# Block 3's statistics on ScalarE, Wv's loads re-cut, evacuations on VectorE and own banks for V in the first segment of a memory-attention and GLU kernel

## The chip, the cores and the metric

One core of a Trainium2 chip runs the kernel. The metric is the device time in microseconds; lower is better. The kernel before ran at 319.13, 319.97 and 320.19 us (median 319.97 us). Its profiled execution took 319.35 us.

Names of engines in the profile: PE is the matrix engine (PEld its weight loads), DVE is VectorE, ACT is ScalarE, POOL is GpSimd, SP issues DMAs. ACT can issue DMAs too (ACTq).

## The reference, cut to what matters

Input x is 2048 tokens by 640 features in bf16. It is normalised over the features, and the result feeds two branches whose outputs are multiplied and added to x:

```
xn = layernorm(x)
# branch A, 32 heads of 20 features, 4 segments of 512 tokens, a memory M, z carried along
q, k, v = xn @ wq, xn @ wk, xn @ wv
per segment: a_dot = softmax(q k^T / sqrt(20) + causal mask) v
             a_mem = phi(q) M / (phi(q) z + 1e-6)
             o     = g * a_mem + (1 - g) * a_dot        # g = sigmoid(beta)
             M += phi(k)^T v ;  z += sum phi(k)
s = o @ wo
# branch B
h = sigmoid(xn @ w_gate) * (xn @ w_up)                  # 640 -> 1536
g = silu(h @ w_down)                                    # 1536 -> 640
out = x + s * g
```

What the change touches is the first step for the first segment alone: the layernorm of its 512 tokens, their transposition, and v = xn @ wv.

## The kernel before, in words

The 2048 tokens are cut into four segments of 512, and each segment into four blocks of 128 tokens (j = 0 to 3; the title's "block 3" is j = 2, "block 4" is j = 3). A tile holds 128 partitions. Matmuls contract over partitions, so each product needs xn transposed: `xnT` holds features on partitions (five chunks of 128) and tokens along the row. A segment needs V (8 products of 128 tokens by 320 columns, five accumulating matmuls each), K and Q (5 products of 128 features by 512 tokens each, again five matmuls each), 12 pairs of gate and up products, scores and attention, and the down products.

For segments 1 to 3 this work is laid into a planner's slots by due times (`TIMES`), far from the change. The first segment's head is written out by hand, in program order, and each engine runs its own instructions strictly in that order. Engines wait for each other through semaphores.

The hand-written head runs as follows (line numbers of the kernel before):

- DMAs are issued from SP and ACT in this order. SP: block 0's left half, block 1, block 2, Wv's right half, Wk, Wq, beta. ACT: block 0's right half, Wv's left half, block 3. Wg and Wu follow on ACT later, in the middle of its work (L144).
- `keep_warm(9)` (L644) runs nine matmuls on zeros while the first block is on its way; a tenth stands after the first transposes.
- For each block: `half_stats0` (L654, L656) is two VectorE `bn_stats` of 320 columns and one `bn_aggr`; the reciprocal standard deviation comes from a ScalarE Sqrt (`root0`, L659) and a VectorE reciprocal (L676) for blocks 0 and 1, and from two GpSimd instructions, add and power (`ln_rstd`, L244 and L245), for blocks 2 and 3; `norm0` (L249) is one VectorE instruction of 640 columns.
- Block 0 is transposed by `first_transpose` (L667) in two pieces of three and two chunks, copied out of PSUM by ScalarE (L672) and VectorE (L670). Blocks 1 to 3 go through `ln_transpose`: five PE transposes (L263) and one copy of 640 columns, on ScalarE for blocks 1 and 2 (L266), on VectorE for block 3 (L268).
- `do_V` runs five matmuls (L130, tile `psv`) and a ScalarE copy into V (L355).
- Then come K (`do_K`, tile `psq`, evacuated by VectorE), Q, the first gates and the slots.

PSUM has eight banks. `Sps`, the scores, holds four of them from the start; the pool `ps_d` of four banks serves everything else, V's products and the transposes included, and each new tile waits for the release of the one four before it.

Of the kernel before, what the change touches and what calls it, by code (L numbers as in the profile page):

```python
# [9 lines left out]
P = 128  # L10
D = 640
# [4 lines left out]
L = 512  # L16
F = 1536
DC = D // P
# [4 lines left out]
HD = D // 2  # L23
# [58 lines left out]
def kernel(  # L82
# [14 lines left out]
    nc = tc.nc  # L97
# [1 line left out]
    o2 = out.flatten_outer_dims()  # L99

    cpool = ctx.enter_context(tc.tile_pool(name="const", bufs=1))
    ps_s = ctx.enter_context(tc.tile_pool(name="ps_s", bufs=1, space=PSUM))
    ps_d = ctx.enter_context(tc.tile_pool(name="ps_d", bufs=4, space=PSUM))
    lnp = ctx.enter_context(tc.tile_pool(name="ln", bufs=2))
    stg = ctx.enter_context(tc.tile_pool(name="stg", bufs=1))
# [13 lines left out]
    ctx.enter_context(tc.manual_schedule(  # L119
        engines={ENG.PE, ENG.Activation, ENG.DVE, ENG.Pool, ENG.SP}))  # L120

    Sps = ps_s.tile([P, 4, L], F32, name="Sps")

    xt_of, xnT_of = {}, {}

# [11 lines left out]
    def load_x(n, a=0, b=4, cols=slice(0, D), eng=nc.sync):  # L137
        if n not in xt_of:
            xt_of[n] = lnp.tile([P, 4, D], BF, name="xt4", bufs=3)
        src = x2[n * L:(n + 1) * L, :].rearrange("(j p) d -> p j d", p=P)  # L140
        eng.dma_start(xt_of[n][:, a:b, cols], src[:, a:b, cols])
# [13 lines left out]
    nc.vector.memset(warm[:, 0:L], 0.0)  # L155
    beta_b = cpool.tile([P, H], BF, name="beta_b")

    def load_wv(half, eng):
        hs = slice(half * HD, (half + 1) * HD)
        eng.dma_start(Wv[:, :, hs], A_wv[:, hs].rearrange("(c p) n -> p c n", p=P))  # L160


    load_x(0, 0, 1, slice(0, HD))
    load_x(0, 0, 1, slice(HD, D), nc.scalar)
    load_x(0, 1, 2)
    load_wv(0, nc.scalar)
    load_x(0, 2, 3)
    load_x(0, 3, 4, eng=nc.scalar)
    load_wv(1, nc.sync)
    load_w(nc.sync, Wk, A_wk)  # L170
    load_w(nc.sync, Wq, A_wq)
    nc.sync.dma_start(beta_b[:], A_beta.partition_broadcast(P))

    epsc = cpool.tile([P, 2], F32, name="epsc")
    nc.gpsimd.memset(epsc[:], EPS)

    nc.scalar.activation(epsc[:, 1:2], epsc[:, 0:1], ACT.Sqrt)
# [69 lines left out]
    def ln_norm(n, j, mv, rs):  # L247
        xn = lnp.tile([P, D], BF, name="xn", bufs=2)
        nc.vector.tensor_scalar(xn[:], xt_of[n][:, j, :], mv[:, j, 0:1], rs[:, j:j + 1],  # L249
                                op0=ALU.subtract, op1=ALU.mult)  # L250
        return xn
# [3 lines left out]
        rs = lnp.tile([P, 4], F32, name="rs")  # L255
        return mv, rs

    def ln_transpose(n, j, xn, eng):
        if n not in xnT_of:
            xnT_of[n] = xpool.tile([P, DC, L], BF, name="xnT")  # L260
        pT = ps_d.tile([P, DC, P], BF, name="pT", tag="d")
        for c in range(DC):
            nc.tensor.transpose(pT[:, c, :], xn[:, c * P:(c + 1) * P], ident[:])  # L263
        dst = xnT_of[n][:, :, j * P:(j + 1) * P]
        if eng is nc.scalar:
            nc.scalar.copy(dst, pT[:])  # L266
        else:
            nc.vector.tensor_copy(dst, pT[:])  # L268

    def ln_spill(n, j, xn):  # L270
        nc.sync.dma_start(Xd[n % 2][j * P:(j + 1) * P, :], xn[:])

# [71 lines left out]
            nc.sync.dma_start(QT[32 * r + DH:32 * r + DH + 3, 4 * half:4 * half + 4, :],  # L344
                              src[r][:, 4 * half:4 * half + 4, :])

    def do_V(n, j, half, evac):
        ps = ps_d.tile([P, HD], F32, name="psv", tag="d")
        for k in range(DC):
            mm(ps[:], xnT_of[n][:, k, j * P:(j + 1) * P], Wv[:, k, half * HD:(half + 1) * HD],  # L350
               k == 0, k == DC - 1)
        dst = V[n % 2][:, j, half * 16:(half + 1) * 16, 0:DH]
        src = ps[:].rearrange("p (h e) -> p h e", e=DH)
        if evac is nc.scalar:
            nc.scalar.copy(dst, src)  # L355
        else:
            nc.vector.tensor_copy(dst, src)
# [290 lines left out]
    new_seg(0)  # L648
    xns, sts = {}, {}

    def half_stats0(j, i):
        if i == 0:
            sts[j] = lnp.tile([P, 2, 6], F32, name="st")
        nc.vector.bn_stats(sts[j][:, i, :], xt_of[0][:, j, i * HD:(i + 1) * HD])  # L654
        if i == 1:
            nc.vector.bn_aggr(mv[:, j, :], sts[j][:])  # L656

    def root0(j):
# [2 lines left out]
    def first_transpose():  # L661

        xnT_of[0] = xpool.tile([P, DC, L], BF, name="xnT")
        for c0, c1 in ((0, 3), (3, 5)):
            pT = ps_d.tile([P, c1 - c0, P], BF, name="pT", tag="d")
            for c in range(c0, c1):
                nc.tensor.transpose(pT[:, c - c0, :], xns[0][:, c * P:(c + 1) * P], ident[:])  # L667
            dst = xnT_of[0][:, c0:c1, 0:P]
            if c0:
                nc.vector.tensor_copy(dst, pT[:])  # L670
            else:
                nc.scalar.copy(dst, pT[:])  # L672

    def norm0(j):
        if j < 2:
            nc.vector.reciprocal(rs[:, j:j + 1], rs[:, j:j + 1])  # L676
        xns[j] = ln_norm(0, j, mv, rs)

    half_stats0(0, 0)
    half_stats0(0, 1)  # L680
    root0(0)
    half_stats0(1, 0)
    norm0(0)
    half_stats0(1, 1)
    half_stats0(2, 0)
    first_transpose()
    root0(1)
    load_w(nc.scalar, Wg, B_w_gate)
    norm0(1)
    half_stats0(2, 1)  # L690
    ln_rstd(mv, rs, slice(2, 3))
    half_stats0(3, 0)
    half_stats0(3, 1)
    ln_rstd(mv, rs, slice(3, 4))
    norm0(2)
    keep_warm(1)
    do_V(0, 0, 0, nc.scalar)
    ln_transpose(0, 1, xns[1], nc.scalar)
    norm0(3)
    late_constants(xns[3])  # L700
    load_w(nc.scalar, Wu, B_w_up)
    do_V(0, 0, 1, nc.scalar)
    do_V(0, 1, 0, nc.scalar)
    ln_transpose(0, 2, xns[2], nc.scalar)
    do_V(0, 1, 1, nc.scalar)
    ln_transpose(0, 3, xns[3], nc.vector)
    do_V(0, 2, 0, nc.scalar)
    do_V(0, 2, 1, nc.scalar)
    do_V(0, 3, 0, nc.scalar)
    do_V(0, 3, 1, nc.scalar)  # L710
    nc.scalar.activation(epsc[:, 1:2], epsc[:, 0:1], ACT.Tanh)
    for c in range(5):
        do_K(0, c, nc.vector)
# [265 lines left out]
```

## Time and profile before

| | |
|---|---|
| median of three runs | 319.97 us (319.13 to 320.19) |
| profiled execution, its own time | 319.35 us |
| its span, first to last instruction | 317.6 us |
| PE busy | 309.7 us, 98% of the span, 4215 matmuls |
| DVE, ACT, POOL busy | 229.5, 227.2, 135.5 us (72%, 72%, 43%) |
| granted clock of PE, mean | 0.999 |
| first matmul on zeros (L644) | 1.24 us |
| first transpose of block 0 (L667) | 5.30 us |
| first V matmul (L130) | 6.37 us |
| first K matmul | 13.35 us |
| first scores (L548) | 35.68 us |

Times inside an execution are counted from the span's start. In a timeline row the first number is the start, the second the time covered, and in brackets stands how long the engine had been idle and what ended that. A busy PE in the profile is modelled (a matmul's end is set by a model of the pipeline), so that starts of matmuls say more than their durations.

### The profile page before, as it was taken

The page shows a single profiled execution, that of the slowest core. Times are in us where ns is not written, and L with a number is a line of the kernel's source. Part 1 is how long each engine was busy: PE and PEld are TensorE (multiplying, and loading weights), DVE is VectorE, ACT ScalarE, POOL GpSimd, SP SyncE. Part 2 cuts the span into 40 slices and gives each one's busy share as a digit, 9 for nine tenths or more (in the row PEclk, how much of TensorE's full clock was granted, in tenths as well). Part 3 has the DMA queues.
Part 4 walks back from the last instruction along what each step waited for, and adds up shares of the span by engine and source line. Part 5 has one row for each costly group of instructions (what it writes and reads, how often), then busy time and mean ns, then how long its engine had stood idle before and what let it go on. Part 6 is the DMA issues. An engine that isn't in the chain of part 4 may idle for free.

```text
span 317.6 us, 10049 instructions
## 1 busy us (share of the span) xinstructions
PE 309.7 (98%) x4215; PEld 167.1 (53%) x4244; DVE 229.5 (72%) x505; ACT 227.2 (72%) x229; POOL 135.5 (43%) x230
## 2 busy tenths in 40 slices
PE   8999999999999999999999999999999999999995
PEld 3544445665555445654665455545466645445673
DVE  6474356755869888997779999977787686734565
ACT  3723477788898877778898868678897766777631
POOL 1870036535263445334453354444533353535322
PEclk9999999999999999999999999999999999999999
DMA  7984886420752462505954443238533000350302
GB/s 252 364 328 142 289 221 191 105 46 2 215 158 62 130 130 85 126 23 173 240 168 122 114 110 109 82 121 210 168 82 120 19 23 23 114 137 4 99 20 83
DMA packets 56085, 41.36 MB, mean 130 GB/s; under 512 B 26952, under 2 KB 54664, under 8 KB 56040
## 3 DMA queue, kind: packets, MB, share of 16 engines
q1 hardware_dynamic: 53496, 35.97, 39.7%
q10 hardware_dynamic: 2544, 4.75, 4.0%
q8 instruction: 33, 0.54, 0.7%
q14 instruction: 12, 0.10, 0.1%
HBM read 19.90 MB, written 14.78 MB: 109 GB/s over the span
## 4 chain that ended last, share of the span: by engine, by line
PE 96%; issue 1%; ACT 1%; DVE 1%; ACTq 0%
PE yp L130 11%; PE up L130 11%; PE gp L130 10%; PE psq L130 10%; PE Sps L548 9%; PE gp L134 6%; PE up L134 6%; PE yp L134 6%; PE psv L130 6%; PE ApsT L572 5%; PE psq L134 4%; PE sp L130 3%; PE sp L134 3%; PE sp L532 2%; PE psv L134 1%; PE wps L644 1%
## 5 line engine op out<-in xcount | busy, mean ns | idle before, releaser
L556 ACT ACTIVATE pt<-Sps 128x2048 bf16<-128x2048 f32 (+1 forms) x81 | 150.3, 1856 | 40.8 <-PE Sps L548 35.9
L558 POOL TENSOR_SCALAR_AFFINE_SELECT pt<-pt 128x512 bf16<-128x512 bf16 x128 | 83.2, 665 | 157.6 <-ACT pt L556 157.5
L438 DVE SCALAR_TENSOR_TENSOR hT<-tg,up 128x512 bf16<-128x512 bf16 x48 | 32.4, 675 | 23.2 <-PE up L130 8.7
L130 PE MATMUL up<-xnT,Wu 128*128 128x512 bf16 x147 | 40.3, 380 | 1.2 <-issue 1.0
L130 PE MATMUL yp<-Wd,hT 128*128 128x320 bf16 x257 | 40.1, 300 | 0.0
L427 ACT ACTIVATE tg<-gp 128x512 bf16<-128x512 f32 x48 | 28.6, 596 | 14.4 <-PE gp L130 11.0
L130 PE MATMUL gp<-xnT,Wg 128*128 128x512 bf16 x144 | 38.1, 379 | 0.3 <-issue 0.2
L548 PE MATMUL Sps<-QT,KT 23*128 23x128 bf16 (+3 forms) x512 | 32.6, 301 | 0.2
L591 DVE STREAM_TRANSPOSE obT<-ob 128x512 bf16<-128x512 bf16 x30 | 21.1, 705 | 13.4 <-POOL ob L587 13.3
L130 PEld LDWEIGHTS <-hT 128*128 128x128 bf16 x257 | 23.5, 98 | 11.6 <-issue 3.0
L455 DVE SCALAR_TENSOR_TENSOR aa<-t,yp 128x320 bf16<-128x320 bf16 x32 | 15.3, 480 | 13.8 <-ACT t L454 13.7
L134 PE MATMUL gp<-xnT,Wg 128*32 128x512 bf16 x360 | 24.1, 380 | 0.0
L548 PEld LDWEIGHTS <-KT 23*128 23x128 bf16 x512 | 10.0, 92 | 24.5 <-issue 24.1
L130 PEld LDWEIGHTS <-Wu 128*128 128x128 bf16 x160 | 14.3, 98 | 16.2 <-issue 3.2
L593 DVE STREAM_TRANSPOSE tb<-ApsT 128x512 f32<-128x512 f32 x30 | 21.2, 708 | 2.2 <-PE ApsT L572 2.1
L572 PE MATMUL ApsT<-pt,V 128*32 128x512 bf16 (+2 forms) x480 | 22.7, 299 | 0.0
L130 PEld LDWEIGHTS <-Wg 128*128 128x128 bf16 x150 | 14.1, 98 | 16.0 <-issue 1.9
L134 PE MATMUL up<-xnT,Wu 128*32 128x512 bf16 x320 | 21.7, 380 | 0.0
L454 ACT ACTIVATE t<-yp 128x320 bf16<-128x320 f32 x32 | 13.9, 435 | 10.2 <-PE yp L130 8.5
L130 PE MATMUL psv<-Wv,xnT 128*128 128x320 bf16 x130 | 20.6, 299 | 0.2
L587 POOL TENSOR_TENSOR ob<-tb,rb 128x320 bf16<-128x320 f32 x27 | 19.8, 733 | 2.3
L134 PE MATMUL yp<-Wd,hT 128*32 128x320 bf16 x508 | 20.0, 300 | 0.0
(122 smaller groups left out, 448.7 us busy)
## 6 DMA issues: line engine op xcount, KB each, us to landing
KT<-Kd SPq DMA_DIRECT2D x32, 80.0 KB
QT<-Qd SPq DMA_DIRECT2D x32, 80.0 KB
out_dram<-xt SPq DMA_DIRECT2D x14, 160.0 KB
Wg<-in_B_w_gate_dram ACTq DMA_DIRECT2D x1, 1920.0 KB
Wu<-in_B_w_up_dram ACTq DMA_DIRECT2D x1, 1920.0 KB
xt<-in_A_x_dram SPq DMA_DIRECT2D x3, 640.0 KB
Wd<-in_B_w_down_dram SPq DMA_DIRECT2D x1, 1920.0 KB
Xd<-xn SPq DMA_DIRECT2D x12, 160.0 KB
```

The lines of the kernel that those rows point to most:

```text
L130: nc.tensor.matmul(out_, lhsT=lhsT, rhs=rhs, start=start, stop=stop, skip_group_check=True)
L134: nc.tensor.matmul(out_[cols], lhsT=lhsT[:, cols], rhs=rhs, start=start, stop=stop, tile_position=(0, 32 * r), skip_group_check=True)
L427: nc.scalar.activation(tg[:], gp[:], ACT.Tanh, scale=0.5)
L438: nc.vector.scalar_tensor_tensor(out=h[:], in0=seg[n]["tg"][:], scalar=1.0, in1=up[:], op0=ALU.add, op1=ALU.mult)
L455: nc.vector.scalar_tensor_tensor(out=s["aa"][j][:, hs], in0=t2[:], scalar=1.0, in1=yp[:], op0=ALU.add, op1=ALU.mult)
L548: nc.tensor.matmul(Sps[:, r, c0:c0 + ncol], lhsT=KT[32 * r:32 * r + DH + 3, g, kb * P:(kb + 1) * P], rhs=QT[32 * r:32 * r + DH + 3, g, q0: ...
L556: nc.scalar.activation(pt[:, :, 0:ntot], Sps[:, :, 0:ntot], ACT.Exp, scale=SCALE)
L558: nc.gpsimd.affine_select(out=pt[:, :, c0:c0 + P], in_=pt[:, :, c0:c0 + P], compare_op=ALU.is_ge, fill=0.0, base=0, pattern=[[0, 4], [1, P ...
L572: nc.tensor.matmul(ps[32 * r:32 * r + 32, q0:L], lhsT=Vflat[n % 2][:, off:off + 32], rhs=t[:, r, c0:c0 + ncol], start=(i == 0), stop=(i == ...
L587: nc.gpsimd.tensor_tensor(ob[:, :, 0:DH], tb[:, :, 0:DH], rb[:].unsqueeze(2).to_broadcast([P, L // 32, DH]), op=ALU.mult)
L591: nc.vector.transpose(s["obT", g // 4][:, g % 4, :], ob[:].rearrange("p b e -> p (b e)"))
L593: s["turn", g] = (lambda: nc.vector.transpose(tb[:].rearrange("p b e -> p (b e)"), ps[:]), quotients, turn_back)
```

## The change

It touches the first segment's head alone.

1. **Loads.** SP now issues block 0's left half, block 1, chunks 0 to 2 of Wv's left half, block 3, Wv's right half, Wk, Wq, beta. ACT issues block 0's right half, block 2, chunks 3 and 4 of Wv's left half. There is one DMA more.
2. **Block 2's statistics** move from VectorE (two `bn_stats`, one `bn_aggr`) and GpSimd (two instructions) to ScalarE: an Identity pass with scale -1/640 whose row sum is the negative mean, a Square pass with that as bias whose row sum is 640 times the variance, and a Sqrt; VectorE takes the reciprocal and normalises. The passes write to a tile of the `aa` pool that nobody reads. A new tile `sums` (two floats) is allocated behind `epsc`.
3. **Block 3's** reciprocal deviation moves from GpSimd to ScalarE (Sqrt) and VectorE (reciprocal).
4. **Evacuations.** The transposes of blocks 1 and 2 are copied out by VectorE in place of ScalarE. Block 0's two pieces are two chunks (ScalarE) and three (VectorE) in place of three and two. Transposition and evacuation are separate calls, so that they can be placed apart in program order.
5. **PSUM.** V's products in the first segment use four banks of their own (`ps_v`); these are given back before `Sps` is allocated in their place.
6. **Order.** On ScalarE the Identity pass stands ahead of block 0's copy, Square and Sqrt behind block 1's Sqrt and ahead of the issue of Wg; block 3's Sqrt stands ahead of the second V copy, Wu's issue behind it. On VectorE the evacuations of blocks 1 and 2 stand between statistics and norms. On PE only the transposes of block 3 move, behind the first V product of block 2.

```diff
-    ps_s = ctx.enter_context(tc.tile_pool(name="ps_s", bufs=1, space=PSUM))
...
-    Sps = ps_s.tile([P, 4, L], F32, name="Sps")
+    first = ExitStack()
+    ps_v = first.enter_context(tc.tile_pool(name="ps_v", bufs=4, space=PSUM))
...
     load_x(0, 1, 2)
-    load_wv(0, nc.scalar)
-    load_x(0, 2, 3)
-    load_x(0, 3, 4, eng=nc.scalar)
+    load_x(0, 2, 3, eng=nc.scalar)
+    load_wv(0, nc.sync, 0, 3)
+    load_wv(0, nc.scalar, 3, DC)
+    load_x(0, 3, 4)
     load_wv(1, nc.sync)
...
     epsc = cpool.tile([P, 2], F32, name="epsc")
+    sums = cpool.tile([P, 2], F32, name="sums")
...
-        for c0, c1 in ((0, 3), (3, 5)):
+        for c0, c1 in ((0, 2), (2, 5)):
...
+    def act_stats(step):
+        if step == 0:
+            sts[2] = fpool.tile([P, D], BF, name="aa", bufs=4)
+            nc.scalar.activation(sts[2][:], xt_of[0][:, 2, :], ACT.Identity, scale=-1.0 / D,
+                                 accum_out=sums[:, 0:1])
+        elif step == 1:
+            nc.scalar.activation(sts[2][:], xt_of[0][:, 2, :], ACT.Square, bias=sums[:, 0:1],
+                                 accum_out=sums[:, 1:2])
+        else:
+            nc.scalar.activation(rs[:, 2:3], sums[:, 1:2], ACT.Sqrt, scale=1.0 / D, bias=epsc[:, 0:1])
...
     half_stats0(0, 0)
     half_stats0(0, 1)
     root0(0)
+    act_stats(0)
     half_stats0(1, 0)
     norm0(0)
     half_stats0(1, 1)
-    half_stats0(2, 0)
     first_transpose()
     root0(1)
+    act_stats(1)
+    act_stats(2)
     load_w(nc.scalar, Wg, B_w_gate)
     norm0(1)
-    half_stats0(2, 1)
-    ln_rstd(mv, rs, slice(2, 3))
     half_stats0(3, 0)
+    keep_warm(1)
+    do_V(0, 0, 0, nc.scalar, ps_v)
+    transpose0(1)
+    evacuate0(1, nc.vector)
+    norm0(2)
     half_stats0(3, 1)
-    ln_rstd(mv, rs, slice(3, 4))
-    norm0(2)
-    keep_warm(1)
-    do_V(0, 0, 0, nc.scalar)
-    ln_transpose(0, 1, xns[1], nc.scalar)
+    root0(3)
+    do_V(0, 0, 1, nc.scalar, ps_v)
+    load_w(nc.scalar, Wu, B_w_up)
+    do_V(0, 1, 0, nc.scalar, ps_v)
+    transpose0(2)
+    do_V(0, 1, 1, nc.scalar, ps_v)
+    evacuate0(2, nc.vector)
     norm0(3)
     late_constants(xns[3])
-    load_w(nc.scalar, Wu, B_w_up)
-    do_V(0, 0, 1, nc.scalar)
-    do_V(0, 1, 0, nc.scalar)
-    ln_transpose(0, 2, xns[2], nc.scalar)
-    do_V(0, 1, 1, nc.scalar)
-    ln_transpose(0, 3, xns[3], nc.vector)
-    do_V(0, 2, 0, nc.scalar)
-    do_V(0, 2, 1, nc.scalar)
-    do_V(0, 3, 0, nc.scalar)
-    do_V(0, 3, 1, nc.scalar)
+    do_V(0, 2, 0, nc.scalar, ps_v)
+    transpose0(3)
+    do_V(0, 2, 1, nc.scalar, ps_v)
+    evacuate0(3, nc.vector)
+    do_V(0, 3, 0, nc.scalar, ps_v)
+    do_V(0, 3, 1, nc.scalar, ps_v)
+    first.close()
+    ps_s = ctx.enter_context(tc.tile_pool(name="ps_s", bufs=1, space=PSUM))
+    Sps = ps_s.tile([P, 4, L], F32, name="Sps")
```

## The prediction

> **What bounds the kernel now.** I read the page first: PE is the chain almost throughout.
>
> ```profile
> span 317.6 us, 10049 instructions
> ...
> PE 309.7 (98%) x4215; PEld 167.1 (53%) x4244; DVE 229.5 (72%) x505; ACT 227.2 (72%) x229; POOL 135.5 (43%) x230
> ...
> PE 96%; issue 1%; ACT 1%; DVE 1%; ACTq 0%
> ```
>
> So what the head gains or loses on PE reaches the end, if nothing later waits for a clock of its own; and only waits of PE can be gained, since the change takes no matmul away (PE's instruction list of the built program keeps its 8490 rows). Next came the timeline of the head. Brackets show PE's weight loader idle, and for whom.
>
> ```profile
> 1.24 4.02 PE L644 MATMUL wps<-mn 128*128 128x512 bf16 x9 [1.24 <-DVE mn L155]
> ...
> 4.15 0.44 DVE L654 BATCH_NORM_STATS2 st<-xt 128x6 f32<-128x320 bf16 x1
> ...
> 4.60 0.16 DVE L676 RECIPROCAL rs<-rs 128x1 f32<-128x1 f32 x1
> 4.80 0.45 DVE L249 TENSOR_SCALAR xn<-xt,mv,rs 128x640 bf16<-128x640 bf16 x1
> ...
> 5.30 0.71 PE L667 MATMUL pT<-ident,xn 128*128 128x128 bf16 x5
> ...
> 5.84 0.48 ACT L672 COPY xnT<-pT 128x384 bf16<-128x384 bf16 x1 [1.28 <-PE pT L667]
> ...
> 6.37 0.52 PEld L130 LDWEIGHTS <-xnT 128*128 128x128 bf16 x5 [0.52 <-ACT xnT L672]
> ...
> 7.24 0.28 PEld L263 LDWEIGHTS <-xn 128*128 128x128 bf16 x5 [0.35 <-DVE xn L249]
> ...
> 7.74 0.69 ACT L266 COPY xnT<-pT 128x640 bf16<-128x640 bf16 x1
> ...
> 8.48 0.52 PEld L130 LDWEIGHTS <-xnT 128*128 128x128 bf16 x5 [0.44 <-ACT xnT L266]
> ...
> 9.38 0.28 PEld L263 LDWEIGHTS <-xn 128*128 128x128 bf16 x5 [0.38 <-DVE xn L249]
> ...
> 10.63 2.88 PE L130 MATMUL psv<-Wv,xnT 128*128 128x320 bf16 x20
> ...
> 13.35 5.56 PE L130 MATMUL psq<-xnT,Wk 128*128 128x512 bf16 x24
> ```
>
> Starts within these rows give PE's pace: a V matmul every 0.136 us, a transpose every 0.056, so 8 x 5 x 0.136 + 15 x 0.056 = 6.28 us of work from the end of the tenth matmul on zeros (6.17, below) to K at 13.35: 7.18 us. The other 0.9 is waiting, at four places: 0.20 for block 0's copy (V starts 6.37), 0.18 for block 1's norm (7.25), 0.27 for its copy (8.48), 0.21 for block 2's norm (9.39). From 9.39 on PE doesn't wait in this head, nor noticeably later: after K starts, the largest idle rows of PE are 0.16 us with no releaser. The ceiling of the change is therefore about 0.87 us, 0.27%.
>
> **The change part by part.** Rules read off the rows: a dependent instruction of another engine starts 0.04 to 0.05 us after its producer's end; an independent one on the same engine about 0.09 before its predecessor's end; a copy can start 0.26 after the start of the last transpose (0.35 at half clock), a V copy 0.335 after the last matmul's start.
>
> *Until block 0's norm* nothing is meant to move, but block 1's load now shares the DMA engines with block 2's (160 KB) on ACT's queue, where Wv's narrow rows were. The trace's landing records have block 1 complete at 4.07, and its statistics start at 4.15, just in time. They stand ahead of the reciprocal on VectorE; ScalarE's Sqrt holds that until 4.60 anyway, which leaves 0.09 us. In the packet records a row of 640 bytes occupies an engine 32 ns, one of 1280 bytes 55 ns. If block 2's packets always interleave, each of block 1's 8 packets per engine waits 23 ns longer: 0.18 us, of which 0.09 reaches everything behind. Bounds: 0 (block 1's packets come first, as they did against Wv's) and 0.3 (block 2's come first). I take 0.08, near the interleaved case. The Trainium skill, DMA: Bandwidth & Descriptors (Queues, rings and completion order; Issuing engines are not separate DMA queues), has an engine take packets from its queues in turn, and says that issuing from several engines saves issue time only; by it the cost would be the 0.09 and Wv on two queues worth nothing by itself. No row here isolates either.
>
> *Block 0's copies.* The first piece has two chunks: its last transpose starts at 5.38, so the copy at 5.73 in place of 5.84; 256 columns on ScalarE take 0.37 in the tail's own row (311.16, L524). It ends at 6.10; the tenth matmul on zeros, begun at half clock, holds PE until 6.17; V starts at 6.18 (before 6.37). The second piece: last transpose 5.70, VectorE free after block 1's aggregate (5.89), since block 2's statistics are gone, so 6.05; 384 columns by interpolation between 0.27 (256) and 0.49 (640): 0.345. Ends 6.40, in time for the third matmul at 6.46.
>
> *Block 2's passes on ScalarE.* The trace has no pass with a row sum. Bounds: the 0.69 of the 640-column copy and, for reading the sum out, the 1.27 of the 1280-column exponential (L371, nearest row of an SBUF-to-SBUF pass). I take 0.75. Identity runs 4.47 to 5.2 (5.75 at the upper end, which would push the first copy by 0.02), behind the Sqrt of block 0 and ahead of the copy at 5.73; queued behind it are that copy and, through it, PE. Its input was the third transfer on SP and is now the second on ACT, so some 0.5 us ahead of its 5.66. Square 6.2 to 6.95, Sqrt to 7.3 (7.9 at the upper end). Queued behind them: Wg's issue (5.93 to about 7.1) and the first V copy (7.26 to about 7.5). Own banks cover that: no PE instruction waits for a V copy until the fifth product needs the first bank, at 9.8.
>
> *Block 1.* Sqrt 6.0 to 6.30, reciprocal 6.34 to 6.50, norm 6.54 to 6.99, transposes at 7.04 (before 7.25), the second V product at 7.32. That needs Wv's right half, complete at 7.19 in the trace after the same 1440 KB; the cover is only 0.1. VectorE's copy 7.53 to 8.02, against ScalarE's 7.74 to 8.43, where it stood behind a V copy and took 0.69: third V product at 8.07 (before 8.48).
>
> *Block 2.* Reciprocal 7.93, norm 8.13 to 8.58, ahead of PE's end of that product at 8.75: the 0.21 goes. Copy 9.23 to 9.72, since block 3's second statistics and aggregate stand ahead of it until 9.21; V at 9.77, 0.06 late.
>
> *Block 3.* Sqrt at 9.25 on ScalarE; the second V copy waits behind it until 9.45 (its bank is next wanted at 10.7). Reciprocal 9.63, norm 9.83 to 10.28, transposes at 10.45, copy 10.94 to 11.43, V at 11.48, 0.07 late; K at 12.84.
>
> *The sum.* Waits left: 0.01 + 0.17 + 0.07 + 0.06 + 0.07 = 0.38 against 0.87; K at 12.84 against 13.35: -0.51. With block 1's load +0.08: **-0.43**.
>
> *What is moved past.* Wk's issue on SP waits for block 0's landing (3.25) through a shared DMA semaphore, so 3.3 in place of 2.66; Wk landed at 9.45 and is wanted at 12.8. Wu's issue slips from 7.75 to about 9.5, but its bytes queue behind Wg's; Wu landed at 23.70 and is wanted at 24.8. The bytes ahead of it are the same and the DMA engines are never idle, so I count 0; if it slid by all of Wg's 1.2 us, 0.1. The last DMAs into QT are issued by 31.9 and the scores start at 35.68; 0.4 less cover costs nothing. GpSimd loses four small instructions (2 x 0.24 + 2 x 0.58) and waits for block 3's norm as before (10.28 against 10.29).
>
> The profiled execution would take 319.35 - 0.43 = 318.92. The median lies 0.62 above the profiled execution; carried along, 319.97 - 0.43 = **319.5 us** (-0.13%).
>
> **The rivals.** What a measurement of this kernel can tell from no change is about 0.3%, 0.96 us.
>
> *All waits go (faster).* If blocks 1 and 2 come without any wait, 0.87 us; and if in addition PE's clock comes up before block 0's transposes, these end 0.25 earlier, and the first V product can start at 6.04: 1.0 us together, 318.95. For: VectorE loses 1.15 us of statistics. Against: 0.17 of wait on block 1's norm hangs on the Sqrt and norm alone. The three times before are 1.06 us apart, so scatter can also carry a gain of 0.4 there.
>
> *The clock comes up late.* Matmuls on zeros start every 0.427 us, later ones of the same width every 0.216 (25 in 5.56): half clock until 6.113 by the clock records, and half again from 316.73:
>
> ```profile
> 316.70:317.60 0.90, 0.00 (x0) 0.00 (x0) 0.00 (x0) 0.00 (x0) 0.00 (x0) 0.51 0.00 0
> ```
>
> The two changes lie 310.613 us apart, 91 times 3.413. If that is a grid with a phase of its own in each execution, the first full step of work after 1.24 ends between 4.65 and 8.06. At 8.06 the first product and block 1's transposes take double: K at 13.6 with the change (13.86 without). Against a median with a typical phase the change then shows as +0.25: 320.2. The Trainium skill, TensorE: Matmul & The Clock Gate (Part 1), states such a free-running window of 3413 ns; the grid in the trace agrees.
>
> *ScalarE's queue holds PE up.* If block 2 lands at 5.66 as before, Identity ends at 6.4, the copy at 6.78, V starts at 6.86 and K at 13.6: 320.2. It decides from a landing of 5.0. Against: it is second on its queue. With a VectorE that keeps PE waiting 0.8 in all, the result is no change, 319.9.
>
> *Everything moves by 32 bytes (slower).* `sums` shifts every later SBUF tile, KT, QT, xnT and x among them, from multiples of 64 bytes to odd multiples of 32. A price of 0.33 ns on each of 4215 matmuls is 1.4 us, and 321.0 after the gain. Against: the products on Mbd, whose chunks begin at such odd places, run at 147 columns in 0.064 us whatever the offset; and `ob`, at an odd multiple of 32 before, is transposed in 0.71 us like the PSUM tile. For: nothing but that DMAs into those tiles aren't shown at such an address. It decides from 0.33 ns.
>
> **How the numbers follow.** Forecast -0.2 to -0.7: 0.53. Late clock: 0.07; ScalarE or VectorE hold PE up: 0.08; both within 0.3%. All waits go, or scatter upon the forecast: 0.20, faster. The shift, or an unseen cost like it: 0.12, slower. So faster 0.20, same 0.68, slower 0.12. The range reaches from a little beyond the full gain (318.7) to the late clock or held-up queue with some scatter (320.4).
>
> **What would show it.** In the changed profile: first V matmul at 6.2 to 6.3, transposes of block 1 at 7.0 to 7.2, third V product at 8.1 to 8.2, no idle before block 2's transposes, K at 12.8 to 13.0, and first scores as much earlier as K. Identity must end before 5.7. Block 0's norm later than 4.80 shows the load's cost. If K starts 0.4 earlier and the scores don't, a DMA (Wu first) took it back. The prediction is wrong if K starts after 13.3, or if the stretch from K to the end is not as long as before.

## The result: 320.57 us after, 319.77 us before, ratio 1.0032

The change makes the kernel slightly slower. Over 17 runs each the median is 320.57 us with the change (319.40 to 322.38) and 319.77 us without (319.13 to 320.39); the ratio is 1.0032, 95% interval 1.0020 to 1.0043. (Ratios here are taken over the runs; they are not the quotient of the two medians, which is 1.0025.) A run more than 1.5% above the fastest of its kernel is left out of a ratio; of all runs below that is one, e7's longest. The prediction was 319.5 us, range 318.7 to 320.4. The profiled execution of the changed kernel took 320.46 us (319.35 before).

First the page of the changed kernel: the span, the engines, SP's DMA queue (packets, MB, share of the 16 DMA engines' time), and the chain.

```profile
span 318.7 us, 10047 instructions
...
PE 309.1 (97%) x4215; PEld 166.8 (52%) x4244; DVE 229.4 (72%) x506; ACT 227.8 (71%) x233; POOL 133.0 (42%) x226
...
q1 hardware_dynamic: 53896, 36.21, 41.6%
...
PE 90%; DMA 3%; ACT 3%; issue 2%; DVE 1%; SPq 1%; POOL 0%; DVEq 0%; ACTq 0%
```

PE has the same 4215 matmuls and is busy no longer than before (309.7 us), in a span that is 1.1 us longer: the loss is waiting, not work. DMA now stands on the chain with 3%; before it was not on it at all. SP's queue, to which the re-cut loads bring 0.24 MB from ACT's, takes 41.6% of the DMA engines' time for 0.7% more bytes; before, its row was:

```profile
q1 hardware_dynamic: 53496, 35.97, 39.7%
```

The timeline of the head after the change, cut to the rows that answer to those of before:

```profile
4.51 0.74 ACT L683 ACTIVATE aa<-xt 128x640 bf16<-128x640 bf16 x1
...
5.16 0.19 ACT L683 ACTIVATION_READ_ACCUMULATOR aa<-xt 128x1 f32 x1
...
5.36 0.45 PE L658 MATMUL pT<-ident,xn 128*128 128x128 bf16 x5 [0.63 <-DVE xn L252]
...
5.68 0.37 ACT L663 COPY xnT<-pT 128x256 bf16<-128x256 bf16 x1 [0.34 <-PE pT L658]
...
5.87 0.34 DVE L661 COPY xnT<-pT 128x384 bf16<-128x384 bf16 x1
...
6.99 0.84 PE L131 MATMUL psv<-Wv,xnT 128*128 128x320 bf16 x5 [0.95 <-DMA Wv<-in_A_wv_dram]
...
7.32 0.49 DVE L645 BATCH_NORM_STATS2 st<-xt 128x6 f32<-128x320 bf16 x1 [0.36 <-DMA xt<-in_A_x_dram]
...
7.66 0.44 PE L670 MATMUL pT<-ident,xn 128*128 128x128 bf16 x5
...
8.48 1.52 PE L131 MATMUL psv<-Wv,xnT 128*128 128x320 bf16 x10 [0.38 <-DMA Wv<-in_A_wv_dram]
...
9.83 0.44 PE L670 MATMUL pT<-ident,xn 128*128 128x128 bf16 x5
...
14.17 0.59 PE L131 MATMUL psq<-xnT,Wk 128*128 128x512 bf16 x2
```

Everything that the prediction computed is there: Identity ends in time, the copies take 0.37 and 0.34, VectorE is early. PE is ready for V at about 6.1, as forecast. Then it waits 0.95 us, for Wv's left half, and again 0.38 for Wv's right half. By the landing records the left half's two pieces are complete at 6.94 (SP) and 6.74 (ACT), against 5.25 for the one piece before; the right half at 8.44 against 7.19; block 3 at 7.29 against 6.04. The third V product starts at 9.15 in place of 8.48. K starts at 13.95 (its first records are missing; reckoned from the last V product at 13.27) in place of 13.35, and the first scores at 36.27 in place of 35.68: **+0.59 us from the head**.

The last matmul starts at 314.75 in place of 313.63, 1.12 us later. So another **0.5 us is lost between the first scores and the end**, where the program is the same. The waits of VectorE for DMAs after 36 us differ (engine, line, what it waited for: us in total, times, longest). Before:

```profile
DVE oT L487 <- DMA oT<-OTd: 1.1, 1, 1.1
...
DVE oTm L518 <- DMA oTm<-Od: 0.5, 1, 0.5
...
DVE aq L320 <- DMA Od<-odot: 0.3, 1, 0.3
```

After:

```profile
DVE oT L478 <- DMA oT<-OTd: 2.3, 2, 1.7
...
DVE qtd L358 <- DMA Qd<-qtd: 0.6, 1, 0.6
...
DVE xn L252 <- DMA Xd<-xn: 0.5, 1, 0.5
```

1.9 us of waits for DMAs have become 3.4, on an engine that runs its instructions in order and feeds PE. These rows don't yet show how PE lost time: its own list of waits after 36 us is the same in both profiles (up 1.0, am 0.3, sp 0.2, gp 0.2, all for "issue").

A finer comparison shows where it went. The 4043 matmuls that follow the first scores are the same ones, in the same order, in both traces, so the lag of each can be followed. By 59 us the changed kernel has gained 0.16 us on before; it loses 0.43 between 165 and 185 us, 0.06 up to 230, and 0.20 at 269. The first of these losses can be followed back, on VectorE and on PE's weight loads:

```profile
165.65 0.79 DVE L358 TENSOR_SCALAR qtd<-qtd 128x1536 bf16<-128x1536 bf16 x1 [0.60 <-DMA Qd<-qtd]
...
168.28 0.49 DVE L446 SCALAR_TENSOR_TENSOR aa<-t,yp 128x320 bf16<-128x320 bf16 x1
```

```profile
168.82 0.50 PEld L131 LDWEIGHTS <-xnT 128*128 128x128 bf16 x4 [0.27 <-issue]
...
179.19 0.76 PEld L131 LDWEIGHTS <-Wu 128*128 128x128 bf16 x5 [0.54 <-DVE odot L407]
```

VectorE waits 0.60 us for the DMA that carries qtd away (in before it doesn't wait there), and its aa, which reads a down product out of PSUM, ends at 168.77 in place of 167.55. The second V product of that place starts 0.05 after it; in before it ran on without a stop. The profile puts this stop down to "issue", but the product waits for a semaphore there, and in four sister profiles (e5, e8, e11, e17) the same stop is put down to aa. At 179 PE waits for VectorE once more.

That left two suspects: the loads at the head, and something that makes DMAs slower all the way through. For the second, `sums` was the candidate: in the built program its 8 bytes take a 32-byte slot, and every SBUF tile allocated later moves by that. Most of the DMAs after the head are relayout DMAs, which carry K, Q, xn and the attention's output through DRAM to change their layout. The tiles that most of them write or read (KT, QT, x, xn, xnT, oT, oTm, obT, ktd) had started at multiples of 256 bytes, and no longer do.

### The profile page after: what moved, and what is told of

Its sections match the earlier page's. It is cut to its first block, busy times and chain, and to the rows that moved or that the text cites. A ratio compares the mean times of both kernels' runs of the same rounds, so it can differ in the third digit from the quotient of the medians.

```text
span 318.7 us, 10047 instructions
## 1 busy us (share of the span) xinstructions
PE 309.1 (97%) x4215; PEld 166.8 (52%) x4244; DVE 229.4 (72%) x506; ACT 227.8 (71%) x233; POOL 133.0 (42%) x226
## 3 DMA queue, kind: packets, MB, share of 16 engines
q1 hardware_dynamic: 53896, 36.21, 41.6%
## 4 chain that ended last, share of the span: by engine, by line
PE 90%; DMA 3%; ACT 3%; issue 2%; DVE 1%; SPq 1%; POOL 0%; DVEq 0%; ACTq 0%
PE up L131 11%; PE gp L131 10%; PE yp L131 10%; PE psq L131 9%; PE Sps L539 8%; PE gp L135 6%; PE up L135 6%; PE ApsT L563 5%; PE yp L135 5%; PE psv L131 4%; PE psq L135 4%; PE sp L131 3%; PE sp L135 3%; ACT pt L547 2%; DMA Wv<-in_A_wv_dram 2%
## 5 line engine op out<-in xcount | busy, mean ns | idle before, releaser
L446 DVE SCALAR_TENSOR_TENSOR aa<-t,yp 128x320 bf16<-128x320 bf16 x32 | 15.3, 478 | 13.3 <-ACT t L445 13.1
```

The lines of the kernel that those rows point to most:

```text
L446: nc.vector.scalar_tensor_tensor(out=s["aa"][j][:, hs], in0=t2[:], scalar=1.0, in1=yp[:], op0=ALU.add, op1=ALU.mult)
```

## The experiments

One table first. "Tiles" says where the tiles just named start, modulo 256 bytes; times of the profiled execution are the first V matmul, the first scores, and the growth of the stretch from there to the last matmul against before; the packet is the mean time of a 1024-byte packet on SP's queue. "All 0" means that qtd, odot, cb and ktok start at multiples of 256 too; the weights start 128 bytes off in every kernel.

| kernel | median us | ratio to before (95%) | tiles | first V | scores | growth | packet ns |
|---|---|---|---|---|---|---|---|
| before | 319.77 | 1 | 0 | 6.37 | 35.68 | 0 | 54.5 |
| after | 320.57 | 1.0032 (1.0020–1.0043) | 32 | 6.99 | 36.27 | 0.52 | 57.4 |
| after, again (e10) | 320.77 | 1.0036 (1.0021–1.0052) | 32 | 6.70 | 36.03 | 1.41 | 57.3 |
| e1 loads alone | 319.48 | 1.0005 (0.9996–1.0015) | 0 | 6.30 | 35.81 | 0.47 | 54.0 |
| e3 Wv on one queue | 321.37 | 1.0079 (1.0052–1.0107) | 32 | 6.89 | 35.72 | 0.48 | 57.9 |
| e6 Wv on SP | 320.20 | 1.0033 (1.0011–1.0055) | 32 | 6.91 | 35.83 | 0.64 | 57.7 |
| e4 no shift | 319.78 | 1.0009 (0.9996–1.0021) | 0 | 6.90 | 36.17 | 0.12 | 54.7 |
| e5 shift alone | 320.21 | 1.0007 (0.9991–1.0023) | 32 | 6.21 | 36.22 | 0.56 | 57.8 |
| e8 shift of 64 | 320.69 | 1.0027 (1.0009–1.0045) | 64 | 7.08 | 37.48 | 0.61 | 57.4 |
| e14 shift of 256 | 319.96 | 1.0009 (0.9997–1.0021) | 0 | 6.73 | 36.03 | 0.26 | 54.6 |
| e7 one queue, no shift | 322.49 | 1.0060 (1.0031–1.0088) | 0 | 8.11 | 38.47 | 0.30 | 55.1 |
| e9 old loads, no shift | 319.28 | 0.9993 (0.9980–1.0006) | 0 | 6.45 | 35.72 | 0.48 | 54.5 |
| e12 old loads, shift | 320.07 | 1.0016 (1.0006–1.0026) | 32 | 6.07 | 35.42 | 1.91 | 58.1 |
| e11 more matmuls on zeros | 320.67 | 1.0040 (1.0025–1.0054) | 32 | 6.80 | 36.20 | 0.72 | 56.7 |
| e13 last block on ScalarE | 319.61 | 1.0010 (0.9995–1.0024) | 0 | 6.16 | 35.36 | 0.06 | 54.5 |
| e15 before, all at 256 | 319.46 | 0.9999 (0.9986–1.0012) | all 0 | 6.37 | 35.78 | −0.01 | 53.5 |
| e16 e13, all at 256 | 319.47 | 0.9995 (0.9983–1.0007) | all 0 | 6.22 | 35.58 | 0.47 | 53.9 |
| e17 e9, all at 256 | 319.34 | 0.9992 (0.9981–1.0004) | all 0 | 6.06 | 35.41 | 0.81 | 53.7 |

The kernels were run in several groups, each beside its own runs of the kernel before and on a chip of its own, so ratios are to be compared, not medians. Before and after have 17 runs each, e11 six, the others eleven or twelve. The growth column is one execution each and scatters as widely as the effect; its mean is 0.86 us over the eight rows with tiles at 32 or 64 and 0.30 over the ten others.

### The loads: e1, e3, e6

e1 puts the change's loads into the kernel before:

```diff
-    load_wv(0, nc.scalar)
-    load_x(0, 2, 3)
-    load_x(0, 3, 4, eng=nc.scalar)
+    load_x(0, 2, 3, eng=nc.scalar)
+    load_wv(0, nc.sync, 0, 3)
+    load_wv(0, nc.scalar, 3, DC)
+    load_x(0, 3, 4)
```

> The kernel before with the change's re-cut loads alone; statistics, evacuations, banks and addresses stay as before. Loads theory (two pieces of Wv's half in flight on two queues are served slowly, 90 to 114 KB in 0.4 us where one queue had 138): first V matmul at 6.8 to 7.2 us in place of 6.37, second V product held until 8.4, K at 13.8 to 14.2, so 320.2 to 320.6 us against about 319.8 for the kernel before. Address theory (the change lost its time later, through the shift by 32 bytes): V as before, K at 13.35, 319.8 us.

The landings moved as the theory says (left half 5.25 to 6.14, right half 7.19 to 8.01), and the time did not (1.0005). The profile shows why it costs so little there: the first V product can't start before 6.30 for block 0's copy anyway; the second waits 0.42 for Wv, but block 2's transposes, which wait for their norm in before, start at 9.41 (9.39 before). Scores come 0.13 late. A later landing costs little while another wait ends after it.

e3 takes the changed kernel and loads Wv's left half as one DMA on ACT, behind block 2; e6 as one DMA on SP, with block 3 on ACT:

```diff
     load_x(0, 2, 3, eng=nc.scalar)
-    load_wv(0, nc.sync, 0, 3)
-    load_wv(0, nc.scalar, 3, DC)
+    load_wv(0, nc.scalar)          # e3, then load_x(0, 3, 4) as it was
+    load_wv(0, nc.sync)            # e6, then load_x(0, 3, 4, eng=nc.scalar)
```

> The changed kernel with Wv's left half in one DMA on ACT's queue, behind block 2; block 3 stays on SP. Loads theory: Wv's halves land by 5.4 and 7.3, first V matmul at 6.2, K at 12.8 to 13.0, 0.9 to 1.0 us earlier than in the changed kernel: 319.3 to 319.7 us. Address theory: K moves as above, but the later growth of 0.5 us stays: 319.8 to 320.2.

> The changed kernel with Wv's left half in one DMA on SP behind block 1, and block 3 on ACT behind block 2. If it is the two queues at once that slow Wv: as with one DMA on ACT, K at 12.8 to 13.0, 319.3 to 319.7 us. If it is that Wv stands behind block 2 or moved at all: Wv late as in the changed kernel, K near 14.0, 320.3 or more.

Neither brought the time back: in both the left half is complete at 6.85 to 6.87, no earlier than in two pieces. What the three forms have in common is that Wv stands third in its queue (issued at 1.71 in each) where it had been second (1.23). In the eight profiles here with the second place the left half is complete between 5.03 and 5.60, in the ten with the third between 6.1 and 8.1. So the place costs even where nothing is cut (e3); cutting over two queues is at most a part. The place is not all, though: block 2's 160 KB ahead of Wv are about 0.5 us at the 361 GB/s below (an estimate), and the left half is 1.5 to 1.7 us late. With the change's loads the DMA engines also move less. The window from 4.0 to 6.8 us, before and after (length, busy time of PE, PEld, DVE, ACT, POOL, granted clock, DMA share, GB/s):

```profile
4.00:6.80 2.80, 2.73 (x13) 1.02 (x12) 2.56 (x10) 0.97 (x3) 0.00 (x0) 1.00 1.11 361
```

```profile
4.00:6.80 2.80, 1.40 (x9) 0.53 (x8) 2.48 (x9) 2.24 (x6) 0.00 (x0) 1.00 0.95 274
```

The eight profiles with before's loads have 352 to 373 GB/s in this window, the ten with the change's place of Wv 257 to 323, the most in e3. Why is not shown. e3 missed its forecast by far, with five of twelve runs above 323 us; e7 (below) shows what most of those are.

### The addresses: e4, e5, e14, e8

e4 is the changed kernel with `sums` in a pool of its own at the end of SBUF, so that nothing else moves; e14 makes `sums` 256 bytes, so that everything moves, but by a whole 256; e8 makes it 64 bytes, to tell odd multiples of 32 from starts off 256; e5 puts a dead 8-byte tile into the kernel before.

```diff
+    endp = ctx.enter_context(tc.tile_pool(name="endp", bufs=1))       # e4
-    sums = cpool.tile([P, 2], F32, name="sums")
+    sums = endp.tile([P, 2], F32, name="sums")                        # e4
+    sums = cpool.tile([P, 64], F32, name="sums")                      # e14
+    sums = cpool.tile([P, 16], F32, name="sums")                      # e8
```

> The changed kernel with the tile of the two sums allocated behind everything else, so that all tiles stand at the addresses of before. Address theory: the head as in the changed kernel (K at about 14.0), but no growth between K and the end: 320.0 to 320.2 us. Loads theory with the later growth as scatter: as the changed kernel, 320.4 to 320.8.

> The changed kernel with the sums' tile grown to 256 bytes, so that all later tiles move by 256 bytes and keep the places they had within 256. If DMAs from or into tiles that lost their start at a multiple of 256 are what costs after K: as the changed kernel at the old addresses, 319.6 to 320.2 us, 1024-byte packets at 54 to 55 ns (57.4 with a shift of 32 or 64), growth between K and the end under 0.5 us. If any move of the tiles costs: 320.4 to 320.9, growth 0.5 to 1.9 us.

> The kernel before with a dead tile of 8 bytes (set once by GpSimd) behind epsc, so that all later tiles stand 32 bytes further, at odd multiples of 32; nothing else changes. Address theory (DMAs into and out of such tiles take longer, VectorE then waits for them in order, and PE loses 0.2 us at a time between K and the end): 320.0 to 320.8 us, with single runs over 321; 1024-byte packets of SP's queue take 55 us of 16 engines in all in place of 52, 4096-byte packets 0.20 us in place of 0.16. Loads or head theory: as before, 319.5 to 319.7.

> The changed kernel with the sums' tile grown to 64 bytes: all later tiles are moved by 64 bytes in place of 32, so they stand at multiples of 64 again, though no longer at those of 256. If odd multiples of 32 are what costs: as without the shift, 319.6 to 320.0 us. If any shift costs (256-byte starts, or the order of tiles): as the changed kernel, 320.3 to 320.8.

e4 came out at 1.0009 where the change has 1.0032, although its head is as late (first V 6.90, scores 36.17); its median is lower than either forecast for it. e14 has the same 1.0009: moving the tiles by a whole 256 costs nothing that can be told. The row of SP's queue on the page (packets, MB, share) says the same. No shift (e4), and a shift of 256 (e14):

```profile
q1 hardware_dynamic: 53896, 36.21, 39.7%
```

```profile
q1 hardware_dynamic: 53896, 36.21, 39.8%
```

With the shift the same packets and bytes took 41.6%. Per packet: 54.5 to 57.4 ns for 1024 bytes. All eight profiles with starts off 256 lie at 56.7 to 58.1 ns, all others at 53.5 to 55.1. The 96 packets of 4096 bytes (QT<-Bd) have a median of 0.159 us before and 0.201 after, but over all profiles the two groups overlap (0.173 to 0.207 with such starts, 0.159 to 0.193 without). The Trainium skill, DMA: Bandwidth & Descriptors (How a descriptor splits into AXI transactions), says that a descriptor which does not start at a multiple of 256 bytes is fetched from the boundary below it, and that the bytes before its start cost time though they aren't used; the trace agrees in sign and in what cures it (e14).

e5 is inconclusive: its packets are slower (57.8 ns), its time is not measurably so (1.0007, with 1.0023 at the upper end, about what the pairs below give for the shift). In its profile block 2 lands at 6.47 in place of 5.66, and VectorE, which waits 0.60 for it, brings block 0's second copy late; one profile doesn't tell whether the shift did that. e8's packets are as slow as with 32 bytes (57.4 ns) and its 1.0027 lies near the change's, which speaks for starts off 256 and against odd multiples of 32; but in its profiled execution, a long one, another trouble lies over it, its clock (below).

### Both undone, one at a time: e9 and e12

e9 is the changed kernel with before's loads, with Identity put behind block 1's Sqrt (block 2 lands later again), and without the shift. e12 is the same with the shift.

```diff
-    load_x(0, 2, 3, eng=nc.scalar)
-    load_wv(0, nc.sync, 0, 3)
-    load_wv(0, nc.scalar, 3, DC)
-    load_x(0, 3, 4)
+    load_wv(0, nc.scalar)
+    load_x(0, 2, 3)
+    load_x(0, 3, 4, eng=nc.scalar)
...
-    act_stats(0)
     half_stats0(1, 0)
...
     root0(1)
+    act_stats(0)
     act_stats(1)
```

> The changed kernel with the loads of before, the sums' tile behind everything else, and the Identity pass moved behind block 1's Sqrt (its block lands at 5.7): statistics on ScalarE, evacuations on VectorE and V's own banks are left. If the prediction's working of the head holds but for the loads and the addresses: first V matmul at 6.2 to 6.3 us, third V product at 8.0 to 8.2, K at 12.8 to 13.0, 319.0 to 319.3 us, ratio 0.998 to 0.999. If the head's chain was misjudged: K at 13.3 or later, 319.6 or more.

> The changed kernel with the loads of before and the Identity pass behind block 1's Sqrt; the tiles stay shifted by 32 bytes. Gate and loads theory (Wv issued behind block 2 comes too late): V at 6.2 to 6.5, K at 12.9 to 13.5, 319.2 to 319.6 us, no run above 320.7. If the shift is what costs: 320.2 or more.

e9 measures 0.9993, e12 1.0016: the same instructions, 0.23% apart through 32 bytes. e9's profiled head missed its forecast, though: block 1 landed at 4.42 (4.07 before) and held the reciprocal of block 0, V starts at 6.45 and K at 13.40, no earlier than before. e12's head is the fastest but two of the whole series, as its timeline shows:

```profile
6.07 0.85 PE L131 MATMUL psv<-Wv,xnT 128*128 128x320 bf16 x5
...
6.97 0.45 PE L669 MATMUL pT<-ident,xn 128*128 128x128 bf16 x5
...
8.97 0.45 PE L669 MATMUL pT<-ident,xn 128*128 128x128 bf16 x5
```

First scores at 35.42, 0.26 ahead of before, and yet it is slower than before. Where its lead goes in this execution can be read from what VectorE and PE wait for in the middle of the run. VectorE's row, from the timeline of e12:

```profile
164.88 0.72 DVE L357 TENSOR_SCALAR qtd<-qtd 128x1536 bf16<-128x1536 bf16 x1 [0.68 <-DMA Qd<-qtd]
```

PE's waits after 36 us in e12 (us in total, times, longest):

```profile
PE psv L131 <- issue: 0.7, 1, 0.7
...
PE Sps L538 <- DMA QT<-Bd: 0.2, 1, 0.2
```

VectorE's wait is there in e9 as well, shorter (0.44). The last row is the scores waiting for a relayout DMA into QT, which neither before nor e9 has. The 0.7 of "issue" has no releaser in the profile; that it comes from the DMAs too is argued, not shown.

Followed matmul by matmul like the changed kernel, all eight profiles with starts off 256 lose 0.43 to 1.86 us between 165 and 185 us (e12 1.86, e10 1.38), and in all eight VectorE waits for Qd<-qtd there, 0.60 to 1.08 us. Of the ten others only e9, e16 and e17 have that wait (0.44 to 1.11) and then the same loss (0.43 to 0.63); five lose nothing. The remaining two, e1 and e7 (0.47 and 0.26), and the excess of e10 and e12 have another stop: PE halts inside a V product, at a matmul that waits for no semaphore, and what it waits for is not known. So the shift makes a loss frequent that can also come without it. The 0.2 us at 269 is in all fourteen profiles of the changed program, shift or none, and in none of the other four; it belongs to the rest of the change, and its cause is open.

### The clock: e7 and e11

e7 is e3 without the shift. It should have been the best form of the changed head.

```diff
-    load_wv(0, nc.sync, 0, 3)
-    load_wv(0, nc.scalar, 3, DC)
+    load_wv(0, nc.scalar)
...
-    sums = cpool.tile([P, 2], F32, name="sums")
+    sums = endp.tile([P, 2], F32, name="sums")
```

> The changed kernel with Wv's left half in one DMA on ACT behind block 2 (as in the run that gave 321.37) and the sums' tile behind everything else, so that no tile is moved. Address theory: the runs at 323 to 324 us vanish, and the median falls to 319.3 to 319.8. If those runs came from the order of the loads: 320.5 or more again.

It is among the slowest, 322.49 us (319.11 to 324.41). PE's timeline and the windows of its profiled execution (length, busy time of PE, PEld, DVE, ACT, POOL, granted clock, DMA share, GB/s) show why for that execution:

```profile
8.11 1.49 PE L132 MATMUL psv<-Wv,xnT 128*128 128x320 bf16 x5 [2.15 <-DMA Wv<-in_A_wv_dram]
9.39 0.74 PE L670 MATMUL pT<-ident,xn 128*128 128x128 bf16 x5
9.93 2.26 PE L132 MATMUL psv<-Wv,xnT 128*128 128x320 bf16 x10
```

```profile
4.60:8.01 3.41, 1.07 (x8) 0.43 (x7) 2.48 (x9) 2.40 (x7) 0.00 (x0) 1.00 1.06 335
8.01:11.42 3.41, 3.31 (x16) 2.16 (x16) 1.21 (x4) 0.43 (x1) 0.00 (x0) 0.50 1.07 383
```

Wv landed at 8.06 here (6.85 for the very same loads in e3's profile). PE idled for most of one window of 3.41 us, and the granted clock was 0.50 for the whole of the next: the wait of 2.15 us is followed by 3.41 us at half speed, and the scores come at 38.47. The Trainium skill, TensorE: Matmul & The Clock Gate (Part 1), describes a window of 3413 ns that runs freely and sets the clock by how busy PE was; the changes at 4.60, 8.01 and 11.42 agree. In e8's profile the clock is full only from 10.48 by the clock records: PE waited for Wv until 7.08, the window from 3.65 to 7.07 with 2.76 of 3.42 us busy did not bring the clock up, and the third V product follows the second by 1.33 us instead of 0.67. It can be close: in the changed kernel's own profile 2.81 of 3.41 us busy (0.64 to 4.05) was followed by the full clock, which stayed through the next window with 1.82 busy. So a head that waits for Wv is not only later, it is exposed to a second loss of over a microsecond.

This profile is one run; the others have their mean granted clock on record. One window at half speed is 0.005 of the span, and e7's profiled run has 0.995. Six of e7's twelve runs have 0.992 to 0.995, four of e3's five above 323 us, e6's two longest, and e13's longest (321.99); every other run has 0.997 or more, the changed kernel's 29 and those of the kernel before among them. A clock that comes up late, as in e8, leaves no mark in this figure (e8's profiled run has 1.000), so it may stand behind other long runs; that isn't shown.

e11 tried to guard the changed kernel against it, with four matmuls on zeros in place of one before V:

```diff
-    keep_warm(1)
+    keep_warm(4)
```

> The changed kernel with four matmuls on zeros in place of one behind block 0's transposes, so that PE has something to do while it waits for Wv. Gate theory (PE's wait of 0.9 to 2 us for Wv leaves a window of 3.41 us too idle, and the clock opens late or closes again): Wv still late and V at 6.9 or later, K at 13.6 to 14.2, but no run above 321.2; median 319.7 to 320.2. Theory that the late Wv costs by its wait alone: as the changed kernel or up to 0.3 slower, with runs above 321.2.

> The changed kernel itself, as measure for the next three. Both theories: 320.2 to 320.9 us, with some runs above 321.2.

It did not help: 1.0040 (six runs, up to 321.69) against 1.0036 for the changed kernel beside it (e10, which repeats the result). With that, the 29 runs without a second drop of the clock, and a clock that came up at 4.05 and 4.47 us in the changed kernel's two profiles (6.11 before), the clock falling back isn't what makes the changed kernel's median.

### Versions that might win: e13, e15, e16, e17

e13 keeps before's loads and addresses, V's own banks and the evacuations on VectorE, and lets ScalarE do the last block's statistics in place of the third's:

```diff
-            sts[2] = fpool.tile([P, D], BF, name="aa", bufs=4)
-            nc.scalar.activation(sts[2][:], xt_of[0][:, 2, :], ACT.Identity, scale=-1.0 / D,
+            sts[3] = fpool.tile([P, D], BF, name="aa", bufs=4)
+            nc.scalar.activation(sts[3][:], xt_of[0][:, 3, :], ACT.Identity, scale=-1.0 / D,
...
```

> Loads and addresses of before; evacuations on VectorE and V's own banks as in the change; ScalarE takes the statistics of the last block (wanted at 9.8 us) in place of the third (wanted at 8.1). If the working of the head is right: no wait of block 2's transposes, third V product at 8.0 to 8.3, K at 12.8 to 13.1, 318.9 to 319.2 us and faster than the kernel before. If VectorE becomes the bound: K at 13.3 or later, 319.5 or more.

Its head is the one that the prediction had drawn; its timeline:

```profile
6.16 1.07 PE L132 MATMUL psv<-Wv,xnT 128*128 128x320 bf16 x5
...
7.20 0.45 PE L670 MATMUL pT<-ident,xn 128*128 128x128 bf16 x5
...
8.93 0.44 PE L670 MATMUL pT<-ident,xn 128*128 128x128 bf16 x5
```

V at 6.16, no wait at block 2, scores 0.32 ahead of before, and the stretch to the end only 0.06 longer: 319.09 us in the profiled execution. Over twelve runs, however, it is 1.0010 (0.9995 to 1.0024), no difference that can be told, and the faster time forecast for it isn't there.

e15 pads three small tiles of the kernel before, so that the tiles that had been 64 or 128 bytes off (qtd, odot, cb, ktok) start at multiples of 256 too; e16 and e17 do the same for e13 and e9:

```diff
-                      kabs=stg.tile([P, DC], F32, name="kabs", bufs=2), hT=[], aa={}, odot=None)
+                      kabs=stg.tile([P, 32], F32, name="kabs", bufs=2)[:, 0:DC], hT=[], aa={}, odot=None)
-        ik = stg.tile([P, DC, H], BF, name="ik")
+        ik = stg.tile([P, 256], BF, name="ik")[:, 0:DC * H].rearrange("p (c h) -> p c h", h=H)
-        dmb = stg.tile([P, DC, WIN], BF, name="dmb")
+        dmb = stg.tile([P, 384], BF, name="dmb")[:, 0:DC * WIN].rearrange("p (c w) -> p c w", w=WIN)
```

> The kernel before with three small tiles padded, so that Q's and the memory's staging tiles (qtd, odot, cb, ktok), which stood 64 or 128 bytes off, start at multiples of 256 too. Address theory: 1024-byte packets fall below 54 ns, and the time by 0.1 to 0.5 us. If 256 is not what matters: no change, within 0.1%.

> The head with the last block's statistics on ScalarE and the loads of before, and all tiles that DMAs touch at multiples of 256. Both theories together: K at 13.0 to 13.1 us, 318.8 to 319.2, faster than the kernel before by 0.1 to 0.2%. If the head's gain is lost to scatter of the loads: as the kernel before.

> The change with the loads of before (Identity behind block 1's Sqrt), and all tiles that DMAs touch at multiples of 256. Both theories together: V at 6.1 to 6.5, K at 13.1 to 13.4 us, 318.9 to 319.3, faster than the kernel before by up to 0.2%. If addresses don't matter beyond the shift: 0.9993 of the kernel before, as without the padding.

Packets get shorter still (53.5 to 53.9 ns), the time doesn't (0.9999, 0.9995, 0.9992; each interval holds 1), against the gains forecast. That the DMAs of the kernel before are hidden but for a little would explain it, but is not shown. No version here beats the kernel before by more than its measurement can tell.

## Why the prediction was wrong

The sum of what the runs show, in parts of the time before (0.1% is 0.32 us):

- **The shift: about +0.25%, 0.8 us.** Changed kernel 1.0032 and 1.0036, without the shift 1.0009 (e4) and 1.0009 (e14). With before's loads, 1.0016 against 0.9993, 0.23%. The intervals of single pairs touch, but all of them point the same way (e3 against e7 too); e5 alone does not show it.
- **The loads: about +0.17%, 0.5 us.** With the shift 1.0034 (mean of after and e10) against 1.0016 (e12), 0.18%; without it 1.0009 (e4) against 0.9993 (e9), 0.16%. These pairs also differ in the place of Identity. The size agrees with the profiles' heads: scores at 36.0 to 36.3 with the change's loads, 35.4 and 35.7 without.
- **All the rest of the change: −0.07%**, 0.9993 (e9), with an interval that holds no change.

The three add up to 0.35%, near the measured 0.32% and 0.36%; that they do is mostly built in, since they are steps from before over e9 and e12 to the change.

By the prediction's own steps:

*Head, engines: right.* ScalarE's copy 0.37 and VectorE's 0.34 (forecast 0.37 and 0.345), Identity 0.74 (0.75), done before the copy (5.35 against 5.68); V's own banks cover the late V copies; no wait at block 2. One instruction was not foreseen as such: each row sum is read out by an instruction of its own of 0.19 us, which overlaps the pass by 0.09. It hid in the slack. In e12 and e13 the first V matmul comes at 6.07 and 6.16 (6.18), block 1's transposes at 6.97 and 7.20 (7.04), and the scores 0.26 and 0.32 ahead, of the 0.51 forecast for PE's waits. Of the rest, e12 loses 0.28 at block 2's norm (transposes at 8.97, PE free at 8.69), which its loads bring late again, and e13 0.16 at block 1's.

*Block 1's load: right.* Forecast +0.08; block 1 landed at 4.24 in place of 4.07, and the norm of block 0 came 0.06 later.

*Wv: the step that failed in the head.* The prediction followed block 1's landing to hundredths and gave Wv's left half no line at all. For the right half it took over the landing "in the trace after the same 1440 KB". But the left half had been second on its queue and ahead of block 2; the change exchanges the two. It landed 1.5 to 1.7 us later, and the first V matmul, which the rest of the change had made ready at 6.1, waited until 6.99. The right half's cover, given as 0.1, was not there either: it landed at 8.44, not 7.19. The sum has +0.08 for block 1's load and nothing for Wv's; what measured was +0.59 at the scores, with all gains already deducted. K at 13.95 is past the 13.3 that the prediction had set as its limit.

*"Everything moves by 32 bytes": the right rival for the wrong reason.* It had the sign and the object, and even its weak point ("DMAs into those tiles aren't shown at such an address"). But it was priced on PE, by 0.33 ns a matmul, and refuted on PE. The price was to be had on the DMA side: 54.5 to 57.4 ns a packet, through VectorE's in-order waits (Qd<-qtd above all) to PE. As priced it came to 321.0 us and a chance of 0.12, and the head's gain was left standing beside it.

*K to the end as long as before: failed,* by 0.5 us in the profiled execution, where the prediction itself had put its other breaking point.

*Clock: rival not needed, but its bounds were wrong.* The clock came up earlier (4.05) in the changed kernel's profile than before (6.11), and it was slower all the same. The prediction let it come up between 4.65 and 8.06, after a step of 3.41 us filled with work; it came up at 4.04 to 4.47 in four profiles, after a step that the matmuls on zeros filled only in part, and at 10.48 in e8.

What stays open: why Wv's left half lands at 6.1 when the change's loads stand in the kernel before (e1) and at 6.7 to 7.1 in the changed kernels, with the same list of DMAs; the landing of one and the same DMA also moved from 6.85 to 8.06 between e3 and e7. Open too is why the DMA engines move fewer bytes with the change's loads. And the way from slower packets to lost time is found at one place (VectorE's wait for Qd<-qtd, 165 to 185 us); the 0.4 to 0.6 us that it mostly takes there, in eight of eight profiles against three of ten, don't add up to the 0.8 us.

## What to carry to other kernels

When loads are re-ordered, write down for each DMA its place in its own queue and its landing, not only the bytes ahead of it, and then ask which consumer the rest of the change has made ready earlier: cover that was ample for the old consumer is not cover for the new one. A small tile allocated ahead of others is part of the change: see whether the tiles behind it that DMAs touch still start at multiples of 256 bytes, or put it at the end. And where PE's first work waits for a load, a late landing can cost twice, once as the wait and once as a clock that falls back.

## What the hardware showed that was not expected

- SBUF tiles that start 32 bytes off a multiple of 256 make 1024-byte packets 5% longer (54.5 to 57.4 ns); all eight profiles with such starts (one of them 64 off) have 56.7 to 58.1 ns, all others 53.5 to 55.1. Moving the tiles by 256 bytes does nothing to them (54.6 ns in e14).
- The same bytes at the head, issued in another order, moved at 274 GB/s in place of 361 between 4.0 and 6.8 us.
- One idle stretch of 2.15 us on PE in the head was followed by 3.41 us at half the granted clock (e7). A window with PE busy for 2.76 of 3.42 us wasn't enough to bring the clock up (e8), one with 2.81 of 3.41 was (after).
- A ScalarE pass with a row sum is two instructions: 0.72 to 0.83 us for 640 columns, and 0.19 us to read the sum.
